# A gate taken straight from PSUM, a new order of seven products, and first weights converted earlier

## The chip, the cores and the metric

The kernel runs on one core of one Trainium2 chip. The metric is the device time of one execution in microseconds; lower is better. TensorE is called PE here, VectorE DVE, ScalarE ACT, GpSimd POOL; SyncE (SP) only starts DMA transfers.

## The reference

Three layers follow each other: causal attention with a decay in place of a softmax, an expert layer with a gate `h * sigmoid(1.702 * h)`, and a second one with a row-wise normalisation.

```python
def _attn_ref(q, k, v):            # (4, 8, 576, 64) each
    scores = scale * np.matmul(q, k.transpose(0, 1, 3, 2))
    gamma = 1.0 - 2.0 ** (-5.0 - np.arange(H, dtype=np.float32))
    Dmat = np.where(rel >= 0, gamma[:, None, None] ** rel[None, :, :], 0.0)
    return np.matmul(scores * Dmat[None], v)

def _moe_ref(x, w_in, w_out):      # 2304 tokens, 512 -> 2048 -> 512
    h = x @ w_in
    g = h * (1.0 / (1.0 + np.exp(-1.702 * h)))
    return g @ w_out

def _moe2_ref(x, w_in, w_out, g_ln):   # 512 -> 1024 -> 512
    h = x @ w_in
    e = np.exp(h - np.max(h, axis=-1, keepdims=True))
    solu = h * (e / (np.sum(e, axis=-1, keepdims=True) + 1e-09))
    ln = (solu - mean(solu)) / np.sqrt(var(solu) + 1e-06) * g_ln
    return ln @ w_out
```

## The kernel before

**Precision.** PE works on fp32r. To keep fp32 accuracy every operand is held as a high part (a cast to fp32r, by ACT) and a low part (the operand minus its high part, by POOL or DVE), and every product is three matmuls: high times high, low times high, high times low. The helper `split` does this: cast on ACT (L293), subtraction (L294), on POOL unless another engine is named.

**Attention** is the first part of the run: eight iterations `k`, two (batch, head pair) units each. POOL multiplies q by its decay (L469, L474), ACT scales v (L484, L488), PE forms scores, states and outputs, DVE masks the scores (L540) and scans the states (L508). Six input buffers are refilled by SP (`load_unit`), and between them SP brings the first pieces of the first expert layer's weights (`load_w`).

**Weights** come as float64. Each piece of 512 columns is turned into fp32 by three integer instructions on DVE (L269, L272, L275, in `convert`). For the input weights four differences of 256 columns (`queue_combine`, L284) follow, and then the split. All this is background work: it stands in a list `bg` with costs, and `slot(n)` takes from it up to a cost of n at fixed points of the program. Pieces marked late (the splits) are put into `late` and run at the next slot.

**The first expert layer** has 24 steps, 4 generations of 512 hidden columns times 3 pairs of 384-token blocks times 2. A step `emit_h` makes a 2 by 2 block of h with seven products of Strassen's kind (Winograd's form) instead of eight. Each product is 6 matmuls of 384 columns, so 42 for a step. The products go to four PSUM banks A, B, C, D, of which A, B and C are used twice: the second product adds onto the first, so PE has to wait until the first has been copied or added away (the copy of A is L678 on ACT, the sum from B is L670 on DVE). Operand sums of x come from `combine_x` and stand in seven tiles `x0` to `x6`, numbered in the order of the products, split high and low; generation 0 makes them and stores them to DRAM, later generations load them back on ACT's DMA queue.

Each of the four outputs then goes through a `gate`: ACT takes the sigmoid (L643), DVE multiplies (L644), ACT casts the high part (L293), POOL subtracts for the low part (L294).

After most steps `emit_y` multiplies gated blocks with the output weights: 48 matmuls of 384 columns (L739), only 24 after each of the first two steps, and once more 48 after the last. The sums are added into SBUF by DVE (L748), in generation 0 copied by ACT.

**In the last generation** the weights of the second expert layer are converted, combined, split and written to DRAM, one 512 KB unit at a time, from two buffers of the tile `ws` (`spill`, L393 to L395). When the first layer's tiles are free (`open_second`), SP fetches these units back, and the second layer begins (`emit_h2`, L803).

**Order.** Nothing is reordered by a scheduler: each engine executes its instructions in the order in which the program emits them.

## Time and profile before

| | us |
|---|---|
| Median of 2 runs | 735.41 (733.69 to 737.13) |
| The profiled execution | 730.73 |
| its span on the chip | 728.9 |
| PE busy | 664.2 (91%) |
| DVE busy | 536.6 (74%) |
| ACT busy | 292.4 (40%) |
| POOL busy | 324.1 (44%) |

The profile is of one execution. Its span is the time from the first instruction to the last; 1.8 us lie around it. [...]

### The profile page before, as it was taken

The numbers are of one execution on the slowest core, as the hardware profiler recorded it, in microseconds if no ns is written. First come the engines' busy times: TensorE is split into PE (matmuls) and PEld (weight loads), VectorE is DVE, ScalarE is ACT, GpSimd is POOL, SyncE is SP. The second block draws the span as 40 slices with busy tenths as digits, with TensorE's granted clock in tenths as the row PEclk, the third lists the DMA queues.
The fourth block names the chain that finished last, engine by engine and source line by source line (L and its number), as shares of the span: only waits on it lengthen the run. The fifth ranks groups of instructions, "written<-read, shape, count | busy, mean of one in ns | idle before, by whom it ended". The sixth has DMA issues, their size and how long they took to land.

```text
span 728.9 us, 11371 instructions
## 1 busy us (share of the span) xinstructions
PE 664.2 (91%) x4326; PEld 613.3 (84%) x4326; DVE 536.6 (74%) x846; ACT 292.4 (40%) x606; POOL 324.1 (44%) x312
## 2 busy tenths in 40 slices
PE   9989577979998989989999998589789999999998
PEld 8988467979998989989999987589468888888887
DVE  3799897976578778788877863657179898777780
ACT  3574335544444332433333332234244454433431
POOL 3578684753555352654435433257114333312300
PEclk9998979989999999999999999789999999999999
DMA  9996256271164762193921647712970000000001
GB/s 352 417 417 281 90 187 231 89 275 56 58 246 160 289 259 85 55 364 117 409 98 58 265 157 282 278 74 100 362 304 15 31 29 15 27 18 30 30 29 44
DMA packets 30006, 121.78 MB, mean 167 GB/s; under 512 B 3328, under 2 KB 3840, under 8 KB 29952
## 3 DMA queue, kind: packets, MB, share of 16 engines
q1 hardware_dynamic: 23904, 88.03, 31.7%
q10 hardware_dynamic: 6048, 33.03, 11.7%
q8 instruction: 34, 0.56, 0.3%
q14 instruction: 20, 0.16, 0.1%
HBM read 88.28 MB, written 32.77 MB: 166 GB/s over the span
## 4 chain that ended last, share of the span: by engine, by line
PE 58%; DVE 22%; DMA 11%; ACT 5%; issue 3%; POOL 2%; SPq 0%; ACTq 0%; POOLq 0%; DVEq 0%
PE y L739 15%; PE o L893 14%; PE h L803 9%; PE h_B L664 4%; PE h_C L664 3%; DVE mem L272 3%; PE h_A L664 3%; DVE mem L284 3%; DVE mem L275 3%; DVE mem L644 2%; DVE mem L269 2%; DMA mem<-in_w2in 2%; PE zT L867 2%; DVE mem L670 2%; PE h_D L664 2%
## 5 line engine op out<-in xcount | busy, mean ns | idle before, releaser
L294 POOL TENSOR_TENSOR g<-mem,g 128x384 fp32r<-128x384 f32 x96 | 109.0, 1147 | 195.7 <-ACT g L293 172.4
L293 ACT CAST g<-mem 128x384 fp32r<-128x384 f32 x96 | 48.5, 514 | 137.7 <-DVE mem L644 137.7
L739 PE MATMUL y<-g,wo 128*128 128x384 f32 x432 | 78.0, 335 | 0.0
L739 PEld LDWEIGHTS y<-g,wo 128*128 128x128 f32 x432 | 75.1, 188 | 0.3 <-DVE mem L748 0.2
L294 POOL TENSOR_TENSOR win<-mem,win 128x256 fp32r<-128x256 f32 (+2 forms) x55 | 49.0, 921 | 58.4 <-ACT win L293 54.4
L644 DVE TENSOR_TENSOR mem<-mem 128x384 f32<-128x384 f32 x72 | 46.7, 676 | 27.1 <-ACT mem L643 27.1
L294 POOL TENSOR_TENSOR ws<-mem,ws 128x512 fp32r<-128x512 f32 (+1 forms) x36 | 41.5, 1166 | 25.1 <-ACT ws L293 25.1
L748 DVE TENSOR_TENSOR mem<-y,mem 128x384 f32<-128x384 f32 x72 | 36.5, 551 | 18.6 <-PE y L739 18.2
L643 ACT ACTIVATE mem<-mem 128x384 f32<-128x384 f32 x72 | 35.5, 520 | 34.2 <-DVE mem L670 31.9
L803 PE MATMUL h<-ut,win 128*128 128x512 f32 x168 | 44.5, 396 | 4.1 <-DMA ut<-wdt 4.1
L809 DVE TENSOR_TENSOR mem<-h,mem 128x512 f32<-128x512 f32 x36 | 24.6, 687 | 31.6 <-PE h L803 17.5
L739 PE MATMUL y<-g,wo1dt.float32r 128*128 128x384 f32 x216 | 42.0, 343 | 2.4 <-ACT g L293 2.4
L670 DVE TENSOR_TENSOR mem<-h_B,mem 128x384 f32<-128x384 f32 x48 | 26.5, 551 | 23.8 <-ACT mem L678 14.8
L272 DVE SCALAR_TENSOR_TENSOR mem<-mem 128x512 uint32<-128x512 uint32 x44 | 42.5, 965 | 1.2
L275 DVE SCALAR_TENSOR_TENSOR mem<-mem 128x512 uint32<-128x512 uint32 x44 | 42.2, 958 | 1.2
L269 DVE TENSOR_SCALAR mem<-mem 128x512 uint32<-128x512 uint32 x44 | 33.7, 767 | 12.3 <-DMA mem<-in_w2in 7.2
L284 DVE TENSOR_TENSOR mem<-mem 128x256 f32<-128x256 f32 (+2 forms) x49 | 41.1, 870 | 2.2 <-POOL x L622 1.4
L854 POOL TENSOR_TENSOR mem<-mem 128x1 f32<-128x1 f32 x18 | 10.3, 572 | 72.8 <-DVE mem L853 66.6
L803 PEld LDWEIGHTS h<-ut,win 128*128 128x128 f32 x168 | 30.8, 188 | 13.3 <-DMA ut<-wdt 6.7
L893 PE MATMUL o<-u,zs 128*128 128x512 f32 (+1 forms) x171 | 41.7, 388 | 0.0
L739 PEld LDWEIGHTS y<-g,wo1dt.float32r 128*128 128x128 f32 x216 | 39.1, 195 | 2.7 <-ACT g L293 2.7
L739 PE MATMUL y<-g,wo0dt.float32r 128*128 128x384 f32 x216 | 40.6, 335 | 0.1
(144 smaller groups left out, 1578.7 us busy)
## 6 DMA issues: line engine op xcount, KB each, us to landing
x<-xd ACTq DMA_DIRECT2D x42, 768.0 KB, 8.3
xd<-x SPq DMA_DIRECT2D x21, 768.0 KB, 4.4
mem<-in_w SPq DMA_DIRECT2D x28, 512.0 KB, 4.8
in<-in_att SPq DMA_DIRECT2D x16, 576.0 KB, 7.8
in<-in_att SPq DMA_DIRECT2D x16, 544.0 KB, 8.2
out<-mem SPq DMA_DIRECT2D x17, 256.0 KB, 2.0
mem<-in_w2out SPq DMA_DIRECT2D x8, 512.0 KB, 3.9
wd<-ws SPq DMA_DIRECT2D x8, 512.0 KB, 6.7
```

Source lines behind the costliest of these rows:

```text
L269: lambda: nc.vector.tensor_scalar(x, high, 3, 0x3FFFFFF8, ALU.logical_shift_left, ALU.bitwise_and),
L272: lambda: nc.vector.scalar_tensor_tensor(high, high, 0xC0000000, x, ALU.bitwise_and, ALU.bitwise_or),
L275: lambda: nc.vector.scalar_tensor_tensor(x, low, 29, high, ALU.logical_shift_right, ALU.bitwise_or),
L284: self.nc.vector.tensor_tensor(o, a, b, ALU.subtract)
L293: self.nc.scalar.copy(hi, src)
L294: (engine or self.nc.gpsimd).tensor_tensor(lo, src, f32(hi), ALU.subtract)
L644: lambda: nc.vector.tensor_tensor(g, src, g, ALU.mult),
L664: nc.tensor.matmul(o, w[:, c:c + P], x[j][:, m, k], start=(start and i == 0), stop=(stop and i == 5), skip_group_check=True,)
L670: add = lambda o, a, b: nc.vector.tensor_tensor(o, a, b, ALU.add)
L739: nc.tensor.matmul(self.yps[m], w[:, c:c + P], gs[:, b], start=(begin and i == 0), stop=(end and i == 2),)
L803: nc.tensor.matmul(o, a[:, l, k], w[:, m], start=(start and i == 0), stop=(stop and i == 5), skip_group_check=True,)
L893: nc.tensor.matmul(o[:, 0:n], z[:, a, k], w[:, b, p * n:(p + 1) * n], start=(k == 0 and i == 0), stop=(k == FB - 1 and i == 2),)
```

## The change

The gate becomes ACT's own function `Gelu_apprx_sigmoid`, evaluated twice from the PSUM bank: once into the high part (which rounds it to fp32r), once in place in the bank. DVE then subtracts the high part from the bank for the low part. POOL and the temporary tiles of the gate are left out.

The seven products come in the order b11, t1, t2, b21, b22, t4, t3, and the x tiles are numbered and made in that order. C's output is summed in its bank, and so are the other two, in D and B.

The first input weights are converted in iterations 2 to 4 of the attention (they were in 4 to 6), and their loads are issued earlier. At most three late pieces run at one slot.

In the last generation the spilled units go through five buffers, two in `ws` and three in a free weight tile (`park`); the list must be empty after the last but one step, with fewer slots to divide it by. The identity's load goes to ACT's queue, ahead of the last fetches.

```diff
 class Build:
     def slot(self, n):
-        late, self.late = self.late, []
+        late, self.late = self.late[:LATE], self.late[LATE:]      # LATE = 3
...
+    def park(self, i):
+        if i % 5 < 2 or i < 2 * NOUT:
+            return self.ws[:, i % 5 if not i < 2 * NOUT else i % 2]
+        i = i % 5 - 2
+        return self.win[2][:, i * SLICE:(i + 1) * SLICE].rearrange("r (a b) -> r a b", a=2)
+
     def spill(self, u, i, src):
-        w = self.ws[:, i % 2]
+        w = self.park(i)
...
-        src = [s2, a11, s1, a12, a21, s2, a22]
+        src = [a11, s1, s2, a12, s2, a22, a21]
...
-    def gate(self, key, src, i):
-        g = self.at(_M["tmp"] + (4 + i) * TW, TW)
...
-        return [
-            lambda: nc.scalar.activation(g, src, AF.Sigmoid, scale=1.702),
-            lambda: nc.vector.tensor_tensor(g, src, g, ALU.mult),
-            lambda: self.split(gs[:, 0], gs[:, 1], g),
-        ]
+        def go(h):
+            nc.scalar.activation(gs[:, 0], h, AF.Gelu_apprx_sigmoid)
+            nc.scalar.activation(h, h, AF.Gelu_apprx_sigmoid)
+            nc.vector.tensor_tensor(gs[:, 1], h, f32(gs[:, 0]), ALU.subtract)
...
+        A = bank("A")
+        mul(A, 0, "b11", True, True)
+        nc.scalar.copy(c11, A)
+        yield 0
+        C = bank("C")
+        mul(C, 1, "t1", True, True)
+        nc.scalar.copy(c22, C)
+        yield 1
         B_ = bank("B")
-        mul(B_, 0, "t2", True, True)
...
+        mul(B_, 2, "t2", True, True)
         add(c12, B_, c11)
         yield 2
         mul(A, 3, "b21", False, True)
-        g11[0]()
-        g11[1]()
-        g11[2]()
+        g11(A)
         self.slot(0)
         yield 3
+        mul(C, 4, "b22", False, True)
+        add(C, C, c12)
+        g12(C)
+        yield 4
+        D_ = bank("D")
+        mul(D_, 5, "t4", True, True)
+        yield 5
+        mul(B_, 6, "t3", False, True)
         add(c21, B_, c11)
...
+        add(D_, D_, c21)
+        add(B_, c22, c21)
         self.done.add(("h", s))
         self.slot(n_slot)
-        g21[1]()
-        g21[2]()
+        g21(D_)
+        g22(B_)
         yield 6
...
-                self.slot((0, 0, 0, 0, 3, 3, 3, 0)[k])
+                self.slot((0, 0, 3, 3, 2.4, 0, 0, 0)[k])
...
-            for _ in range((0, 1, 1, 1, 1, 1, 1, 0)[k]):
+            for _ in range((2, 0, 0, 1, 1, 1, 1, 0)[k]):
                 load_w()
             if k > 3:
-                make_x(*((1, 3), (0, 2), (4, 6), (5,))[k - 4])
+                make_x(*((0, 3), (1, 2), (5, 6), (4,))[k - 4])
         self.open_right()
-        self.slot(5)
+        self.slot(6)
...
-            slots = max(1, 2 * (5 - s % 6 - (g == GENS - 1)) + 2 - (g == GENS - 1))
+            slots = max(1, 2 * (5 - s % 6) + 2 - 4 * (g == GENS - 1))
...
             if s == NSTEP - 2:
+                assert not self.bg and not self.late
...
+        nc.scalar.dma_start(out=self.at(IDENT_AT, P), in_=self.ident_in)
...
-        self.load(IDENT_AT, self.ident_in)
```

On PE, the seven products of one step in the third generation (h_A to h_D are the banks, x_126 to x_132 the tiles x0 to x6), before:

```order
L664 MATMUL h_B<-x_126,win0dt.float32r 128x384 x6
L664 MATMUL h_A<-x_127,win0dt.float32r 128x384 x6
L664 MATMUL h_C<-x_128,win0dt.float32r 128x384 x6
L664 MATMUL h_A<-x_129,win0dt.float32r 128x384 x6
L664 MATMUL h_B<-x_130,win0dt.float32r 128x384 x6
L664 MATMUL h_C<-x_131,win0dt.float32r 128x384 x6
L664 MATMUL h_D<-x_132,win0dt.float32r 128x384 x6
```

and with the change:

```order
L672 MATMUL h_A<-x_126,win0dt.float32r 128x384 x6
L672 MATMUL h_C<-x_127,win0dt.float32r 128x384 x6
L672 MATMUL h_B<-x_128,win0dt.float32r 128x384 x6
L672 MATMUL h_A<-x_129,win0dt.float32r 128x384 x6
L672 MATMUL h_C<-x_130,win0dt.float32r 128x384 x6
L672 MATMUL h_D<-x_131,win0dt.float32r 128x384 x6
L672 MATMUL h_B<-x_132,win0dt.float32r 128x384 x6
```

B moves from first to third place and its second product from fifth to last; A's and C's second products now have two products between them and the first, where A had one.

On DVE, a step of the second generation from the last conversion ahead of it (L670, now L678, are the sums from the banks, L644 the gate's multiplication, L652 the gate's subtraction, L275 or L276 a conversion), before:

```order
L275 SCALAR_TENSOR_TENSOR mem<-mem 128x512
L670 TENSOR_TENSOR mem<-h_B,mem 128x384
L644 TENSOR_TENSOR mem<-h_A,mem 128x384
L670 TENSOR_TENSOR mem<-h_B,mem 128x384
L670 TENSOR_TENSOR mem<-mem 128x384
L670 TENSOR_TENSOR mem<-h_C,mem 128x384
L644 TENSOR_TENSOR mem<-mem 128x384 x2
L670 TENSOR_TENSOR mem<-h_D,mem 128x384
L280 TENSOR_SCALAR mem<-mem 128x512
L269 TENSOR_SCALAR mem<-mem 128x512
```

and with the change:

```order
L276 SCALAR_TENSOR_TENSOR mem<-mem 128x512
L678 TENSOR_TENSOR mem<-h_B,mem 128x384
L652 TENSOR_TENSOR g_1081<-h_A,g_1081 128x384
L678 TENSOR_TENSOR h_C<-h_C,mem 128x384
L652 TENSOR_TENSOR g_1082<-h_C,g_1082 128x384
L678 TENSOR_TENSOR mem<-h_B,mem 128x384
L678 TENSOR_TENSOR h_D<-h_D,mem 128x384
L678 TENSOR_TENSOR h_B<-mem 128x384
L281 TENSOR_SCALAR mem<-mem 128x512
L270 TENSOR_SCALAR mem<-mem 128x512
```

The sums of C, D and B now end in their banks, and each gate still has one DVE instruction, now with one operand in PSUM; the count stays at nine for a step. The conversions keep their places, ahead of the first sum and behind the last.

On POOL, the end of the attention (L469 and L474, now L477 and L482, are the decays of the last two units in_72 and in_73; L622, now L630, the low parts of x; win0 the first input weights), before:

```order
L622 TENSOR_TENSOR x_127<-mem,x_127 128x384 x2
L622 TENSOR_TENSOR x_129<-mem,x_129 128x384 x2
L469 TENSOR_TENSOR in_72<-in_72,qdec 128x64
L469 TENSOR_TENSOR in_73<-in_73,qdec 128x64
L474 TENSOR_TENSOR in_72<-in_72,qdec 128x512
L474 TENSOR_TENSOR in_73<-in_73,qdec 128x512
L622 TENSOR_TENSOR x_126<-mem,x_126 128x384 x2
L622 TENSOR_TENSOR x_128<-mem,x_128 128x384 x2
L294 TENSOR_TENSOR win0dt.float32r<-mem,win0dt.float32r 128x768
L294 TENSOR_TENSOR win0dt.float32r<-mem,win0dt.float32r 128x512 x2
L622 TENSOR_TENSOR x_130<-mem,x_130 128x384 x2
L622 TENSOR_TENSOR x_132<-mem,x_132 128x384 x2
```

and with the change:

```order
L295 TENSOR_TENSOR win0dt.float32r<-mem,win0dt.float32r 128x768
L295 TENSOR_TENSOR win0dt.float32r<-mem,win0dt.float32r 128x512 x2
L630 TENSOR_TENSOR x_126<-mem,x_126 128x384 x2
L630 TENSOR_TENSOR x_129<-mem,x_129 128x384 x2
L477 TENSOR_TENSOR in_72<-in_72,qdec 128x64
L477 TENSOR_TENSOR in_73<-in_73,qdec 128x64
L482 TENSOR_TENSOR in_72<-in_72,qdec 128x512
L482 TENSOR_TENSOR in_73<-in_73,qdec 128x512
L630 TENSOR_TENSOR x_127<-mem,x_127 128x384 x2
L630 TENSOR_TENSOR x_128<-mem,x_128 128x384 x2
L630 TENSOR_TENSOR x_131<-mem,x_131 128x384 x2
L630 TENSOR_TENSOR x_132<-mem,x_132 128x384 x2
```

The first weights' subtractions move from behind the decays of the last two units to ahead of the first x.

## Rows read from the trace of the kernel before

**Rows 1.** Stretches: busy us of each engine (instructions), granted clock, DMA share, GB/s.

```profile
69.10:189.10 120.00, 96.26 (x495) 91.88 (x494) 96.54 (x127) 54.47 (x106) 73.13 (x57) 0.91 0.42 154
189.10:419.30 230.20, 222.05 (x1261) 219.67 (x1261) 182.42 (x281) 89.91 (x179) 111.64 (x89) 0.99 0.51 192
419.30:514.30 95.00, 78.21 (x409) 75.70 (x408) 54.04 (x93) 30.73 (x64) 42.13 (x40) 0.91 0.48 180
```

**Rows 2.** Waits of PE: us in total, times, longest.

```profile
PE h_B L664 <- DVE mem L670: 18.7, 9, 6.7
PE y L739 <- ACT g L293: 8.8, 3, 3.2
PE h_A L664 <- ACT mem L678: 8.6, 5, 3.4
PE h_B L664 <- ACT win1dt.float32r L293: 6.5, 1, 6.5
PE h L803 <- DMA ut<-wdt: 4.1, 8, 2.0
```

**Rows 3.** Timeline of PE: start, us, operation; beginnings of steps, end of the last.

```profile
69.10 1.31 PE L664 MATMUL h_B<-x,win0dt.float32r 128*128 128x384 f32 x6
...
115.60 1.40 PE L664 MATMUL h_B<-x,win0dt.float32r 128*128 128x384 f32 x6
...
173.49 1.20 PE L664 MATMUL h_B<-x,win1dt.float32r 128*128 128x384 f32 x6
...
189.09 1.20 PE L664 MATMUL h_B<-x,win 128*128 128x384 f32 x6
...
436.81 1.20 PE L664 MATMUL h_B<-x,win1dt.float32r 128*128 128x384 f32 x6
...
512.03 2.25 PE L739 MATMUL y<-g,wo1dt.float32r 128*128 128x384 f32 x12
```

**Rows 4.** Groups of DVE by shape: busy, mean ns, idle before.

```profile
L644 DVE TENSOR_TENSOR mem<-mem 128x384 f32<-128x384 f32 x72 | 46.7, 676 | 27.1 <-ACT mem L643 27.1
L272 DVE SCALAR_TENSOR_TENSOR mem<-mem 128x512 uint32<-128x512 uint32 x44 | 42.5, 965 | 1.2
...
L670 DVE TENSOR_TENSOR mem<-h_B,mem 128x384 f32<-128x384 f32 x48 | 26.5, 551 | 23.8 <-ACT mem L678 14.8 <-PE h_B L664 8.9
...
L644 DVE TENSOR_TENSOR mem<-h_A,mem 128x384 f32<-128x384 f32 x24 | 13.3, 552 | 19.0 <-ACT mem L643 19.0
```

**Rows 5.** Timeline of DVE: the same conversion beside POOL's work, and without it.

```profile
72.13 1.39 DVE L272 SCALAR_TENSOR_TENSOR win1dt.uint<-win1dt.uint,mem 128x512 uint32<-128x512 uint32 x1
...
84.83 0.69 DVE L272 SCALAR_TENSOR_TENSOR wo3dt.uint<-wo3dt.uint,mem 128x512 uint32<-128x512 uint32 x1
```

**Rows 6.** The page's groups: the subtraction of every gate on POOL.

```profile
L294 POOL TENSOR_TENSOR g<-mem,g 128x384 fp32r<-128x384 f32 x96 | 109.0, 1147 | 195.7 <-ACT g L293 172.4
```

**Rows 7.** Groups of ACT by shape.

```profile
L293 ACT CAST ws<-mem 128x512 fp32r<-128x512 f32 x22 | 13.1, 618 | 21.5 <-DMA wdb<-ws 14.9 <-DMA wdt<-ws 6.7
L643 ACT ACTIVATE mem<-h_A 128x384 f32<-128x384 f32 x24 | 11.8, 492 | 14.4 <-PE h_A L664 14.4
```

**Rows 8.** Timeline of POOL: last decays, first weights, last splits of x.

```profile
53.88 2.49 POOL L474 TENSOR_TENSOR in<-in,qdec 128x512 f32<-128x512 f32 x2
...
63.00 4.29 POOL L294 TENSOR_TENSOR win0dt.float32r<-mem,win0dt.float32r 128x768 fp32r<-128x768 f32 x3 [1.89 <-ACT win0dt.float32r L293]
67.25 8.53 POOL L622 TENSOR_TENSOR x<-mem,x 128x384 fp32r<-128x384 f32 x6
```

**Rows 9.** Timeline of PE where the second layer begins.

```profile
516.25 0.97 PE L803 MATMUL h<-ut,win 128*128 128x512 f32 x3 [1.98 <-DMA ut<-wdt]
...
533.32 1.54 PE L803 MATMUL h<-ut,ws 128*128 128x512 f32 x6
...
543.23 1.06 PE L867 MATMUL zT<-mem 128*128 128x128 f32 x8 [1.57 <-DMA mem<-in_ident]
```

**Rows 10.** Timeline of DVE: the end of tile 0's normalisation.

```profile
540.25 0.81 DVE L856 TENSOR_SCALAR mem<-mem 128x1024 f32<-128x1024 f32 x1 [0.67 <-POOL mem L854]
```

More of the change, by code (lines that the diff above doesn't have):

```diff
@@ L632, in load_x, with gate @@
         self.nc.scalar.dma_start(out=x, in_=self.xd[p][j])
-    def gate(self, key, src, i):
+    def gate(self, key):
         nc = self.nc
-        g = self.at(_M["tmp"] + (4 + i) * TW, TW)
         slot = self.gfree.pop(0)
+        self.gt[key] = slot
         gs = self.gs[slot]
-        self.gt[key] = slot
-        return [
-            lambda: nc.scalar.activation(g, src, AF.Sigmoid, scale=1.702),
-            lambda: nc.vector.tensor_tensor(g, src, g, ALU.mult),
-            lambda: self.split(gs[:, 0], gs[:, 1], g),
-        ]
+        def go(h):
+            nc.scalar.activation(gs[:, 0], h, AF.Gelu_apprx_sigmoid)
+            nc.scalar.activation(h, h, AF.Gelu_apprx_sigmoid)
+            nc.vector.tensor_tensor(gs[:, 1], h, f32(gs[:, 0]), ALU.subtract)
+        return go
     def emit_h(self, s, n_slot):
@@ L672, in emit_h @@
         c11, c12, c21, c22 = (self.at(_M["tmp"] + i * TW, TW) for i in range(4))
-        B_ = bank("B")
-        mul(B_, 0, "t2", True, True)
-        yield 0
-        A = bank("A")
-        mul(A, 1, "b11", True, True)
-        nc.scalar.copy(c11, A)
+        f = 2 * n
+        g11, g12, g21, g22 = (self.gate((g, p, t, f + c)) for t in range(2) for c in range(2))
+        A = bank("A")
[6 more added lines that the diff above has]
+        yield 1
+        B_ = bank("B")
+        mul(B_, 2, "t2", True, True)
         add(c12, B_, c11)
-        yield 1
-        C = bank("C")
-        mul(C, 2, "t1", True, True)
-        nc.scalar.copy(c22, C)
         yield 2
         mul(A, 3, "b21", False, True)
-        f = 2 * n
-        if not self.gfree:
-            raise ValueError(s)
-        g11, g12 = self.gate((g, p, 0, f), A, 0), self.gate((g, p, 0, f + 1), c12, 1)
-        g21, g22 = self.gate((g, p, 1, f), c21, 2), self.gate((g, p, 1, f + 1), c22, 3)
-        g11[0]()
-        g11[1]()
-        g11[2]()
+        g11(A)
         self.slot(0)
         yield 3
-        mul(B_, 4, "t3", False, True)
-        add(c21, B_, c11)
-        add(c22, c22, c21)
-        yield 4
-        mul(C, 5, "b22", False, True)
-        add(c12, C, c12)
-        g22[0]()
-        g12[0]()
-        g12[1]()
-        g12[2]()
-        g22[1]()
-        yield 5
-        D_ = bank("D")
-        mul(D_, 6, "t4", True, True)
-        add(c21, D_, c21)
-        g22[2]()
-        g21[0]()
+        mul(C, 4, "b22", False, True)
[6 more added lines that the diff above has]
+        mul(B_, 6, "t3", False, True)
+        add(c21, B_, c11)
+        add(D_, D_, c21)
+        add(B_, c22, c21)
         self.done.add(("h", s))
         self.slot(n_slot)
-        g21[1]()
-        g21[2]()
+        g21(D_)
+        g22(B_)
         yield 6
```

3 lines of the change are left out of this document (2 added, 1 removed).

## The prediction

> **What bounds the kernel now.** I read the stretches first, then the waits of PE, then the timelines of PE, DVE and POOL where those waits lie. In the first expert layer PE is the engine with the most work, but it is not kept busy everywhere: in the first generation (69.1 to 189.1 us) it is busy 96.3 of 120 us at a mean granted clock of 0.91, and DVE is busy just as long, 96.5 us; in the long middle it is busy 222 of 230 us; in the last 95 us it is busy 78.2, again at 0.91, while DVE has only 54 us of work [rows 1]. So one stretch is short of DVE, one is short of something that DVE, ACT and PE all wait for, and the middle is nearly full.
>
> The beginnings of the steps give the size of it [rows 3]. One undisturbed step lasts 189.09 - 173.49 = 15.60 us for 42 + 48 matmuls, 0.173 us each. Against that I count what each stretch has too much:
> - first two steps, each with 24 matmuls of y (4.16 us) fewer: 115.60 - 69.10 = 46.5 us for 22.9, too much 23.6;
> - next three steps: 57.9 us for 46.8, too much 11.1;
> - fifteen steps from 189.09 to 436.81: 247.7 us for 234.0, too much 13.7;
> - the last three, with the closing 48 matmuls (8.3 us), to 512.03 + 2.25 = 514.28: 77.5 us for 55.1, too much 22.4.
> Together 70.8 us. The listed waits are the larger part of it [rows 2]; the rest I put down to matmuls at the lower of the two clock levels, by the 0.91 of the two stretches that hold most of the waits, and let it shrink with the waits.
>
> A fifth piece lies where the second layer begins [rows 9]. From 514.28 to the first transposes at 543.23 are 28.95 us. The last 36 of the 78 matmuls in it run without waiting, from 533.32 to 543.23 - 1.57 = 541.66, so 0.23 us each or 18.0 us for all: too much 10.9, while each unit is fetched back from DRAM.
>
> **What the change does, part by part.**
>
> *POOL loses the gates.* 96 subtractions of 1.147 us, 109 us of POOL [rows 6]. What counts is DVE: the same conversion takes 1.39 us beside POOL and 0.69 without [rows 5], and the 44 of one kind average 0.965, so 44 x 0.275 = 12 us of this one of three conversion instructions is waiting for POOL [rows 4]. The three kinds together have lost some 35 us by that measure (an estimate from the one kind). The gates are a third of POOL's 324 us, so some 12 us of DVE time come back, about 4 of them in the first generation.
>
> *DVE's own gate work.* 72 multiplications at 0.676 us become subtractions with one operand in PSUM; the nearest row is the first gate's multiplication, which also reads a bank, at 0.552 [rows 4]. That is 72 x 0.124 = 8.9 us less, 2 us of it in the first generation. The five sums stay at 0.55 as long as writing a bank costs what reading one does; no row shows DVE writing a bank here, so I bound it by 0.55 and by twice that, 72 x 0.55 = 40 us spread over 24 steps, 1.65 us each, and take the lower end, since the nearest row (a sum from a bank, 0.551) is of the same size and shape. [...]
>
> *ACT* keeps ten instructions a step: four sigmoids and four casts become eight evaluations. The nearest row is the sigmoid read from a bank, 0.492 us [rows 7]; ACT is at most 45% busy in any stretch [rows 1], so even at double that price (2 us more a step) it stays covered. I take nothing for it. The wait it adds: the subtraction stands behind two ACT passes in a row, 0.98 us, where the multiplication stood behind one. Behind it in DVE's order are the next sum and then conversions. For the first two gates the next sum has to wait for PE's next product (1.04 us) anyway, and for the last two the conversions come first. I take 2 us for all, and keep up to 94 for the rivals.
>
> *The order of the products.* PE waited 18.7 us for the sum from B, queued on DVE behind conversions, and 8.6 for the copy of A [rows 2]. B's second product now comes two products later, at six products from the step's start instead of four, so DVE has 2.08 us more; A's copy has 1.04 more. Of the waits for B all but the longest are below 3 us, so most vanish; the same order gives the second gate two products more before y needs it, which concerns the 8.8 us of y.
>
> *First weights earlier.* Iterations 4 to 6 had eleven DVE pieces of it and now have the four differences: seven conversions leave the crowded end, six for iterations 2 and 3, one for the slot right behind the attention. At 0.69 to 1.39 us each [rows 5] that would give 5 to 10 us. But POOL does not get less: its decays end at 56.37, and it works on the first weights (4.29 us) and the six last subtractions of x until 75.78 with 1.89 idle [rows 8], and step 0 can't finish before x is split. The weights now go ahead of the last decays, which may delay the last attention iteration by 4.3 us. The ends are 4 us lost and 7 gained; I take 2 gained, the idle POOL time, since POOL's order is what ends last there. The loads only change places within one queue of DMAs, three of them are issued ahead of the last attention inputs in both versions, so nothing for that.
>
> *Spills.* In the last generation ACT waited 21.5 us for the two `ws` buffers to be written out [rows 7], and everything behind it in ACT's order with it: gates, copies of A, issues of x loads. With five buffers the first five spills of each half wait for nothing. All are done a step earlier, so the fetches no longer stand behind them in SP's queue, and the closing 96 matmuls (16.6 us) cover the fetches.
>
> **The sum**, against the profiled 730.73 us:
> - first two steps: 23.6 to 13. The second step's weights still have to be converted after the first step's sums, and DVE has no spare time there: 10.6 off;
> - next three: 11.1 to 4: 7.1 off;
> - middle: 13.7 to 4.5 (longest waits 3 us against 2.08 us of room, and x loads that no edit touches): 9.2 off;
> - last three: 22.4 to 7: 15.4 off;
> - beginning of the second layer: 10.9 to 2: 8.9 off. Late next is tile 0's normalisation, ready at 541.06 [rows 10], only 0.6 us ahead of PE's 541.66, hence the 2;
> - attention: 2 off; added wait for ACT: 2 on.
> 51.2 us off, 679.5 for a profiled run. The median stands 4.7 above that execution, and 735.4 - 51.2 gives **684 us**. With the bounds (first five steps saving 8 to 28 instead of 17.7, the last three and the second layer 16 to 30 instead of 24.3, the middle 4 to 12, attention -4 to 7) the forecast's own range is 664 to 706.
>
> **The rivals.**
>
> 1. *The first generation stays as it is.* DVE and POOL both do the x splits there, DVE's work is 96.5 us, and I free only some 6 of it; the waits might just move to x. Then the 17.7 us of the first five steps and half of the middle's 9.2 are missing: 735.4 - 29 = 706 us. For it speaks DVE as busy as PE; against it, that the longest waits are for single sums and gates. Chance 0.13.
>
> 2. *The spills stay the bound.* DVE's conversions there also wait for loads which SP starts only behind the first half's spills, and seven spills still follow each other within one step, at most three to a slot; if that order, not the buffers, sets the pace, the 24.3 us of the end are missing: 735.4 - 27 = 708 us. For it: DVE has 41 idle us in the last 95 [rows 1]. Against it: ACT's 21.5 us name the buffers. Chance 0.08.
>
> 3. *No real change:* each removed wait is replaced by one of like size, within 2% of 735. Chance 0.05.
>
> 4. *Slower: DVE is tied to ACT.* DVE executes in order, and each of its 96 subtractions now waits for two ACT passes. If DVE had nothing to cover any of them, it would idle 96 x 2 x 0.492 = 94 us, against 27.1 + 19.0 = 46 now [rows 4]: 48 us more. If these reached PE in full and only the gains of the end stayed (24 us), the time would be 735 + 48 - 24 = 759 us. DVE has 445 - 333 = 112 us idle in the three stretches [rows 1], so this decides only if most of the added waits fall where DVE is behind, that is in the first generation and right after a conversion. Chance 0.04.
>
> **Chances and range.** The forecast has 0.70. 2% of 735 (14.7 us) is about what a measurement here can tell from no change. Forecast and the first two rivals are faster by more than that, 0.91, of which I give 0.01 to smaller gains: faster 0.90, same 0.06, slower 0.04. The range has to take in the two middle rivals to leave out no more than 2 in 10: 664 to 710.
>
> **What would show it.** POOL's busy time falls by about 109 us and the conversions' mean from 0.965 towards 0.8; the waits of PE for the sum from B fall from 18.7 us to under 6; the second step starts at about 85 us instead of 90; the last three steps take about 62 us; no wait for fetched units, and transposes about 19 us after the last product of y; the granted clock is above 0.95 in the first and last stretch. Wrong would be: a DVE subtraction above 0.7 us, an ACT evaluation above 0.8, or PE waiting for x or for DVE subtractions in the first generation as long as it waited before.

## The result, and the profile after

The changed kernel takes **697.02 us** (median of 2 runs, 696.78 to 697.27) against 735.41: a ratio of 0.948, 95% interval 0.938 to 0.957. The forecast was 684, its range 664 to 710. The profiled execution took 697.27, its span is 695.5 us.

The table cuts both spans at the beginnings of the steps in the timeline of PE and sets the predicted saving beside the measured one (us).

| stage | before | after | predicted | measured |
|---|---|---|---|---|
| up to step 0 (attention) | 69.1 | 66.1 | -2 | -3.0 |
| steps 0 and 1 | 46.5 | 45.8 | -10.6 | -0.7 |
| steps 2 to 4 | 57.9 | 54.7 | -7.1 | -3.2 |
| steps 6 to 20 | 247.7 | 240.5 | -9.2 | -7.2 |
| steps 21 to 23 with the closing y | 77.5 | 69.5 | -15.4 | -8.0 |
| from there to the first transpose | 29.0 | 17.6 | -8.9 | -11.4 |

The measured column adds up to the 33.5 us between the two profiled executions. The medians are 38.4 apart, since the profiled run of before was 4.7 below its own median. The long middle and the second layer came out about as foreseen; the first five steps and the last three gave about half or less. (One execution of the variant "conversions ahead" below, the one that its trace is of, took 1366 us; it is left out of that variant's median, and its stages are not given.)

Stretches of the profile after, which answer [rows 1]; the columns are the same.

```profile
66.10:182.20 116.10, 96.71 (x494) 93.30 (x493) 86.27 (x128) 51.70 (x106) 43.64 (x33) 0.90 0.47 170
182.20:406.90 224.70, 220.68 (x1261) 219.81 (x1261) 149.48 (x281) 82.26 (x179) 47.20 (x33) 0.99 0.53 196
406.90:492.10 85.20, 73.69 (x411) 72.24 (x410) 50.02 (x93) 29.27 (x65) 25.33 (x23) 0.94 0.73 282
66.07:111.88 45.81, 30.99 (x135) 28.46 (x134) 42.40 (x55) 20.16 (x39) 26.26 (x20) 0.80 0.53 204
```

DVE (the third pair of numbers) has 33 us less work in the middle, where it was no bound, and 10 less in the first generation. The last row is steps 0 and 1 alone: DVE is busy 42.4 of 45.8 us there, PE only 31.0, at a mean granted clock of 0.80. The same two steps before:

```profile
69.10:115.60 46.50, 29.79 (x134) 26.70 (x133) 41.46 (x50) 18.95 (x34) 34.06 (x25) 0.86 0.41 161
```

POOL had 7.8 us more work there than with the change, but DVE had about the same: 41.5 us. None of the 10 us came out of these two steps. The granted clock is the share of the full one: in windows of 0.2 us, one every 0.5 us up to 690, it is 1.00 in 1302, 0.50 in 72 and between these in 6 (before: 1280, 91 and 9). So the lower of the prediction's two levels is 0.50.

The waits of PE, as in [rows 2].

```profile
PE h_B L672 <- DVE mem L678: 15.2, 4, 9.6
PE h_A L672 <- ACT win1dt.float32r L294: 5.0, 1, 5.0
PE h_B L672 <- DMA x<-xd: 3.2, 2, 1.7
PE h_B L672 <- DVE g L652: 2.9, 1, 2.9
PE h_A L672 <- POOL win1dt.float32r L295: 2.6, 1, 2.6
...
PE y L736 <- POOL wo3dt.float32r L295: 2.2, 1, 2.2
...
PE h_A L672 <- ACT mem L685: 1.3, 1, 1.3
```

Waits for the sum from B are fewer (4, not 9). The longest, 9.6 us, is in step 22, where PE had waited 6.7 us before as well. DVE and PE at that place before, DVE waiting for a load ahead of the sum:

```profile
468.41 0.43 DVE L269 TENSOR_SCALAR mem<-mem 128x512 uint32<-128x512 uint32 x1 [4.43 <-DMA mem<-in_w2in]
...
472.21 2.29 PE L664 MATMUL h_B<-x,win0dt.float32r 128*128 128x384 f32 x6 [6.74 <-DVE mem L670]
```

Waits for the copy of A, for gates ahead of y and for fetched units are gone or nearly so.

Groups of DVE and ACT by shape (busy, mean ns, idle before), which answer [rows 4] and [rows 7].

```profile
L273 DVE SCALAR_TENSOR_TENSOR mem<-mem 128x512 uint32<-128x512 uint32 x44 | 32.1, 730 | 1.2
L678 DVE TENSOR_TENSOR h_B<-mem 128x384 f32<-128x384 f32 x24 | 14.5, 603 | 0.0
L652 DVE TENSOR_TENSOR g<-h_C,g 128x384 fp32r<-128x384 f32 x24 | 13.4, 558 | 23.1 <-ACT h_C L651 23.1
L678 DVE TENSOR_TENSOR h_C<-h_C,mem 128x384 f32<-128x384 f32 x24 | 13.3, 555 | 0.0
L652 DVE TENSOR_TENSOR g<-h_A,g 128x384 fp32r<-128x384 f32 x24 | 13.3, 554 | 20.8 <-ACT h_A L651 20.8
L652 DVE TENSOR_TENSOR g<-h_D,g 128x384 fp32r<-128x384 f32 x24 | 13.2, 551 | 1.5 <-ACT h_D L651 1.5
L652 DVE TENSOR_TENSOR g<-h_B,g 128x384 fp32r<-128x384 f32 x24 | 13.2, 549 | 1.2 <-ACT h_B L651 1.2
L651 ACT ACTIVATE h_A<-h_A 128x384 f32<-128x384 f32 x24 | 11.7, 489 | 0.0
```

The prices hold: a subtraction from PSUM 0.55 us, an evaluation on ACT 0.49, a sum written into a bank 0.555 (0.603 with both operands in SBUF). The conversion in the first row falls from 965 to 730 ns.

The timeline of PE at the places that the prediction named; it answers [rows 3] and [rows 9].

```profile
66.07 1.34 PE L672 MATMUL h_A<-x,win0dt.float32r 128*128 128x384 f32 x6
...
85.21 0.69 PE L672 MATMUL h_A<-x,win1dt.float32r 128*128 128x384 f32 x1 [5.03 <-ACT win1dt.float32r L294]
88.51 1.97 PE L672 MATMUL h_A<-x,win1dt.float32r 128*128 128x384 f32 x5 [2.62 <-POOL win1dt.float32r L295]
...
99.90 1.87 PE L672 MATMUL h_B<-x,win1dt.float32r 128*128 128x384 f32 x6 [2.73 <-DVE mem L678]
...
455.18 2.29 PE L672 MATMUL h_B<-x,win0dt.float32r 128*128 128x384 f32 x6 [9.60 <-DVE mem L678]
...
489.98 2.24 PE L736 MATMUL y<-g,wo1dt.float32r 128*128 128x384 f32 x12
492.06 1.55 PE L800 MATMUL h<-ut,win 128*128 128x512 f32 x6
...
509.78 1.03 PE L864 MATMUL zT<-mem 128*128 128x128 f32 x8
```

Step 1 starts at 85.21, as predicted, but it then takes 26.7 us, against 25.6 before (89.98 to 115.60), where it began so:

```profile
89.98 0.69 PE L664 MATMUL h_B<-x,win1dt.float32r 128*128 128x384 f32 x1 [6.51 <-ACT win1dt.float32r L293]
```

The second layer follows y without a gap, and no unit is waited for.

Two timelines of DVE in the same trace hold what went wrong. The first is the way into step 1:

```profile
67.09 1.40 DVE L273 SCALAR_TENSOR_TENSOR win1dt.uint<-win1dt.uint,mem 128x512 uint32<-128x512 uint32 x1
...
74.09 0.55 DVE L678 TENSOR_TENSOR mem<-h_B,mem 128x384 f32<-128x384 f32 x1
...
82.21 1.55 DVE L285 TENSOR_TENSOR mem<-mem 128x256 f32<-128x256 f32 x4
...
84.95 2.38 DVE L621 TENSOR_TENSOR mem<-mem 128x768 f32<-128x768 f32 x1
87.37 3.85 DVE L285 TENSOR_TENSOR mem<-mem 128x768 f32<-128x768 f32 x2
...
96.48 2.90 DVE L630 TENSOR_TENSOR x<-mem,x 128x384 fp32r<-128x384 f32 x2
99.30 0.54 DVE L678 TENSOR_TENSOR mem<-h_B,mem 128x384 f32<-128x384 f32 x1
...
448.71 0.43 DVE L270 TENSOR_SCALAR mem<-mem 128x512 uint32<-128x512 uint32 x1 [8.46 <-DMA mem<-in_w2in]
```

Apart from three waits of 2.8 us together, DVE works through from 64.8 to 111.9: conversions until 74.1, step 0's sums and gates, conversions and the four differences of the next weights until 83.7, then x sums, conversions and an x split ahead of step 1's first sum from B. The last row is the other place: in step 22 DVE waits 8.46 us for one of the two last float64 pieces of the spills, and the sum that PE needs stands behind it, as it did before behind a wait of 4.43.

### The profile page after: what moved, and what is told of

It reads as the page before. It is cut to its first block, busy times and chain, and to the rows that moved or that the text cites. A ratio compares the mean times of both kernels' runs of the same rounds, so it can differ in the third digit from the quotient of the medians.

```text
span 695.5 us, 11232 instructions
## 1 busy us (share of the span) xinstructions
PE 651.9 (94%) x4326; PEld 609.2 (88%) x4326; DVE 485.6 (70%) x846; ACT 279.2 (40%) x606; POOL 213.2 (31%) x216
## 4 chain that ended last, share of the span: by engine, by line
PE 68%; DMA 6%; DVE 4%; ACT 1%; issue 1%; POOL 0%; ACTq 0%; DVEq 0%
PE y L736 22%; PE o L890 14%; PE h L800 12%; PE h_B L672 5%; PE h_A L672 5%; PE h_C L672 5%; DMA x<-xd 4%; PE h_D L672 3%; PE zT L864 2%; DMA mem<-in_w2in 1%; DVE mem L273 1%; DVE mem L276 0%; DVE mem L270 0%; DVE x L630 0%; DVE g L652 0%
## 5 line engine op out<-in xcount | busy, mean ns | idle before, releaser
L295 POOL TENSOR_TENSOR win<-mem,win 128x256 fp32r<-128x256 f32 (+2 forms) x63 | 58.6, 960 | 114.7 <-ACT win L294 80.6
L678 DVE TENSOR_TENSOR mem<-h_B,mem 128x384 f32<-128x384 f32 x48 | 26.5, 551 | 32.3 <-PE h_B L672 30.2
L685 ACT COPY mem<-h_A 128x384 f32<-128x384 f32 x24 | 11.6, 483 | 84.7 <-PE h_A L672 84.7
L890 PE MATMUL o<-wo,zs 128*128 128x512 f32 (+1 forms) x171 | 40.0, 378 | 0.0
L630 POOL TENSOR_TENSOR x<-mem,x 128x384 fp32r<-128x384 f32 x30 | 34.6, 1180 | 17.5 <-ACT x L628 17.5
L736 PEld LDWEIGHTS y<-g,wo0dt.float32r 128*128 128x128 f32 x216 | 37.7, 188 | 0.0
L672 PE MATMUL h_B<-x,win0dt.float32r 128*128 128x384 f32 x108 | 23.8, 358 | 13.7 <-DVE mem L678 10.8
L890 PEld LDWEIGHTS o<-wo,zs 128*128 128x128 f32 x171 | 31.0, 188 | 6.0
L276 DVE SCALAR_TENSOR_TENSOR mem<-mem 128x512 uint32<-128x512 uint32 x44 | 34.5, 785 | 1.2
L890 PEld LDWEIGHTS o<-u,zs 128*128 128x128 f32 x171 | 29.9, 189 | 5.1
L270 DVE TENSOR_SCALAR mem<-mem 128x512 uint32<-128x512 uint32 x44 | 20.7, 469 | 18.4 <-DMA mem<-in_w2in 10.6
```

Of the source, the lines that this page charges most:

```text
L270: lambda: nc.vector.tensor_scalar(x, high, 3, 0x3FFFFFF8, ALU.logical_shift_left, ALU.bitwise_and),
L276: lambda: nc.vector.scalar_tensor_tensor(x, low, 29, high, ALU.logical_shift_right, ALU.bitwise_or),
L295: (engine or self.nc.gpsimd).tensor_tensor(lo, src, f32(hi), ALU.subtract)
L630: (engine or self.nc.gpsimd).tensor_tensor(x[:, 1, k], a[:, k], f32(x[:, 0, k]), ALU.subtract)
L672: nc.tensor.matmul(o, w[:, c:c + P], x[j][:, m, k], start=(start and i == 0), stop=(stop and i == 5), skip_group_check=True,)
L678: add = lambda o, a, b: nc.vector.tensor_tensor(o, a, b, ALU.add)
```

## Experiments

Ratios are to the kernel before, from runs on the same chip as each experiment; medians are of two to six executions, and each row's stages come from one trace. The stages, cut as above:

| kernel | median us | ratio, 95% interval | step 0 at | 0 and 1 | 2 to 4 | 6 to 20 | 21 to 23 |
|---|---|---|---|---|---|---|---|
| change | 697.02 | 0.948 (0.938 to 0.957) | 66.1 | 45.8 | 54.7 | 240.5 | 69.5 |
| first weights late | 699.0 | 0.951 (0.947 to 0.955) | 69.5 | 43.1 | 52.6 | 240.6 | 69.2 |
| old gate | 711.3 | 0.968 (0.965 to 0.971) | 65.6 | 50.7 | 62.5 | 238.5 | 73.1 |
| old order | 703.37 | 0.957 (0.952 to 0.962) | 68.4 | 45.7 | 54.0 | 241.8 | 71.7 |
| old gate and order | 719.5 | 0.981 (0.976 to 0.985) | 66.4 | 51.1 | 57.8 | 251.1 | 72.5 |
| two spill buffers | 699.49 | 0.952 (0.948 to 0.956) | 65.6 | 46.0 | 52.6 | 240.8 | 71.5 |
| no x loads at the end | 691.01 | 0.942 (0.935 to 0.949) | 65.5 | 45.9 | 54.2 | 240.9 | 60.4 |
| last pieces later | 695.87 | 0.949 (0.945 to 0.953) | 66.1 | 45.3 | 53.9 | 240.4 | 68.9 |
| no low parts of x | 692.85 | 0.943 (0.939 to 0.947) | 64.2 | 42.5 | 54.2 | 239.5 | 70.5 |
| conversions ahead | 696.37 | 0.948 (0.945 to 0.952) | | | | | |
| casts later | 689.92 | 0.938 (0.935 to 0.940) | 65.6 | 45.9 | 52.7 | 240.5 | 62.8 |
| casts and pieces | 688.23 | 0.935 (0.932 to 0.938) | 71.6 | 39.9 | 51.4 | 238.8 | 62.9 |
| fewer at step 0 | 688.55 | 0.937 (0.935 to 0.940) | 70.7 | 35.9 | 56.1 | 240.1 | 62.8 |

In every row with stages the first transpose comes 17.6 us after the last product of y.

**1. The first weights late again.**

```diff
-                self.slot((0, 0, 3, 3, 2.4, 0, 0, 0)[k])
+                self.slot((0, 0, 0, 0, 3, 3, 3, 0)[k])
-            for _ in range((2, 0, 0, 1, 1, 1, 1, 0)[k]):
+            for _ in range((0, 1, 1, 1, 1, 1, 1, 0)[k]):
-        self.slot(6)
+        self.slot(5)
```

> The changed kernel with the first weights' conversions and loads back in iterations 4 to 6 of the attention (all else as changed). The first step started 3.0 us earlier after the change (66.07 against 69.10 us) and the second step 4.8 us earlier, but the third only 3.7. Theory A (the early conversions gave those 3 us, as DVE is the end of the attention's chain): first step at about 69 us and 3 to 5 us slower than the changed kernel, about 701 us. Theory B (POOL's splits of x end the stretch whatever DVE does): no change beyond 1 us, about 697 us.

Step 0 starts 3.4 us later, but step 2 starts at 112.6, against 111.9. So the early weights bring the start forward and lose it again before step 2. The median, 699.0, lies between the two expected, and the interval contains the change's ratio.

**2. The gate and the order of the products, each undone alone and both together.** The gate's edit:

```diff
...
         def go(h):
-            nc.scalar.activation(gs[:, 0], h, AF.Gelu_apprx_sigmoid)
-            nc.scalar.activation(h, h, AF.Gelu_apprx_sigmoid)
-            nc.vector.tensor_tensor(gs[:, 1], h, f32(gs[:, 0]), ALU.subtract)
+            nc.scalar.activation(g, h, AF.Sigmoid, scale=1.702)
+            nc.vector.tensor_tensor(g, h, g, ALU.mult)
+            self.split(gs[:, 0], gs[:, 1], g)
```

> The changed kernel with the gate of before (sigmoid by ACT, product by DVE, cast by ACT, subtraction by POOL), the first, third and fourth gate's input being the bank; order of the products, early weights and buffers as changed. Theory A (the gate gives DVE its time back, since POOL's 96 subtractions slowed DVE's conversions): conversions' mean back from 0.73 to about 0.95 us, waits for the sum from B in the middle return, 8 to 15 us slower than the changed kernel, 705 to 712 us. Theory B (the order of the products took the middle's waits away, the gate only saves idle engines' time): within 3 us, 697 to 700 us.

The order's edit puts back the sequence t2, b11, t1, b21, t3, b22, t4, with its x tiles and the sums where it needs them (the gate stays new):

```diff
+        mul(B_, 0, "t2", True, True)
...
-        mul(A, 0, "b11", True, True)
+        mul(A, 1, "b11", True, True)
...
-        mul(B_, 6, "t3", False, True)
...
+        mul(D_, 6, "t4", True, True)
```

> The changed kernel with the order of the seven products of before (t2, b11, t1, b21, t3, b22, t4) and the x tiles numbered for it; gate, early weights and buffers as changed. Theory A (the later place of B's second product gives DVE 2.08 us of room in each step): PE waits again for the sum from B in the middle, 6 to 12 us slower, 703 to 709 us. Theory B (faster conversions alone would have ended those waits): within 3 us, 697 to 700 us.

With both edits:

> The changed kernel with both the gate and the order of the products of before; early weights, buffers and the list's deadlines as changed. The middle (fifteen steps from step 6 on) lasted 240.5 us in the changed kernel, 238.5 with the gate alone of before, 241.8 with the order alone of before, and 247.7 before. Theory A (either of the two is enough to end the middle's waits for the sum from B): the middle is back at 245 to 248 us, the whole at 718 to 724 us. Theory B (something else of the change ended them): the middle stays at 239 to 242 us, the whole at about 713 to 717 us.

The gate is worth 14.3 us in the new order (711.3 - 697.0) and 16.1 in the old one (719.5 - 703.4); the order 6.4 and 8.2, of which the 6.4 lies within the two intervals' overlap (0.948 and 0.957) and is not clear of noise. What remains, 733.6 - 719.5 on one chip or some 14 us, is the rest of the change. By the traces it is 2.7 at the start of step 0, 5.0 in the last three steps and 11.4 at the second layer's start, less 4.6 us in steps 0 and 1 and 3.4 in the middle, which take longer there than in the kernel before.

The gate's worth does not lie where it was expected. In the new order, undoing it makes steps 0 and 1 4.9 us longer, steps 2 to 4 7.8 and the last three 3.6, but not the middle, whose waits were to return: it is 2.1 shorter. In steps 0 and 1 DVE is as busy as in the change (42.0 us); PE waits there for the splits of weights by ACT and POOL, 9.2 and 8.9 us, against 5.7 and 4.8 in the change. The old gate's subtractions stand in POOL's order among these splits.

In the middle the gate and the order do the same work: without both the steps 6 to 20 take 251.1 us, with either alone 241.8 or 238.5. The waits of PE without both, over the whole run (lines after the gate stand 3 later there):

```profile
PE h_B L675 <- DVE mem L681: 29.3, 12, 11.4
```

Of these, eight waits of 11.2 us together are in the middle (7.9 before, none in the change); the one of 11.4 is in step 22.

The three conversions of the same shape with the old gate alone, in groups of DVE:

```profile
L276 DVE SCALAR_TENSOR_TENSOR mem<-mem 128x512 uint32<-128x512 uint32 x44 | 39.8, 905 | 1.2
L273 DVE SCALAR_TENSOR_TENSOR mem<-mem 128x512 uint32<-128x512 uint32 x44 | 35.8, 814 | 1.2
...
L270 DVE TENSOR_SCALAR mem<-mem 128x512 uint32<-128x512 uint32 x44 | 26.2, 595 | 13.5 <-DMA mem<-in_w2in 7.7 <-DMA mem<-in_w2out 5.0 <-DMA mem<-in_w 0.8
```

Their sum is 2.31 us there, against 1.98 in the change (785, 730, 469) and 2.69 before (958, 965, 767). Over 44 of each, the old gate, with its work on POOL, thus cost DVE's conversions 15 us, not quite half of the fall of 31; the rest came with the other edits.

**3. Two spill buffers instead of five.**

```diff
-        w = self.park(i)
+        w = self.ws[:, i % 2]
```

> The changed kernel with all spills through the two ws buffers again. Theory A (the buffers gave the earlier end of the spills, and with it the covered fetches): ACT waits for the buffers again, last three steps and beginning of the second layer 10 to 20 us longer, 707 to 717 us. Theory B (the earlier deadline for the list gave it, and DMA bandwidth sets the pace of the last steps anyway): within 4 us, 697 to 701 us.

Only 2 us come back in the last three steps, less than the medians can tell, and the second layer's start doesn't change. The three new buffers, on which the prediction built, are not what removed the waits for fetched units. The spills' earlier deadline is what is left of the edit at this place, with the identity's load on another queue; neither was undone alone. The order in SP's queue speaks for the deadline. Timelines of SP, the last spills and the first fetch, before and with the change:

```profile
506.91 4.01 SPq L395 DMA_DIRECT2D wdt<-ws  x2
511.02 1.15 SPq L210 DMA_DIRECT2D ut<-wdt  x2
```

```profile
463.53 1.57 SPq L403 DMA_DIRECT2D wdt<-ws  x2
465.19 1.29 SPq L211 DMA_DIRECT2D ut<-wdt  x2
```

In both the first fetch is issued right behind the last spill, but before that was 3 us ahead of the end of y, and now it is 27 (25 with two buffers). The identity's load was issued behind all fetches (at 534.36), so it can have caused only the 1.57 us that the transposes waited for it.

**4. The last x loads left out.**

```diff
-                        self.load_x(after, j)
+                        if g < GENS - 1 or at + 2 < NPR:
+                            self.load_x(after, j)
```

> The changed kernel without the x loads for the last pair of the last generation (seven loads of 768 KB; the last two steps compute with the pair before's x). In the changed kernel DVE waited 8.46 us for the last two float64 pieces, loaded from 438.2 us on and there at 448.7, while those x loads and the spills were moving, and PE waited 9.6 us for DVE in step 22. Theory A (the transfers are late because the x loads are ahead of them): the pieces arrive 4 us or more earlier, PE's wait falls below 4 us, the last three steps take 63 us instead of 69.5. Theory B (the pieces are issued late by SP, behind DVE's conversions, and the x loads don't matter): the wait stays above 7 us.

Timeline of DVE without these loads, at the conversion that had waited 8.46 us:

```profile
440.66 0.43 DVE L270 TENSOR_SCALAR mem<-mem 128x512 uint32<-128x512 uint32 x1 [1.00 <-DMA mem<-in_w2in]
```

The wait is 1.00 us, PE's wait at that place 3.1 instead of 9.6, and the last three steps take 60.4 us, 9 less. In the change both float64 pieces of 512 KB are issued from 438.2 us on, behind seven x loads of 768 KB that were issued from 424 to 434; there they land after 10.8 us (the median of the two), here after 5.2. They are also issued 3.1 us earlier here (435.1): in the change SP waited 3.9 us for a spill to be written. So the x loads make the pieces late, most of it in the transfer and some of it in the issue.

**5. Mending the end.** First the conversions of the last two pieces behind step 22's first gate:

```diff
         g11(A)
-        self.slot(0)
+        self.slot(99 if s == NSTEP - 2 else 0)
...
-            self.slot(6 if s == 0 else self.left() // max(1, slots) if s + 2 < NSTEP else 0)
+            self.slot(6 if s == 0 else self.left() // max(1, slots) if s + 3 < NSTEP else 0)
+            if s == NSTEP - 2:
+                self.slot(0)
```

> The changed kernel with the conversions of the last two float64 pieces moved from ahead of step 22's first sum to behind its first gate's subtraction, so that DVE's wait for them no longer stands ahead of the sum that PE waits for. Theory A (PE's 9.6 us in step 22 are DVE's order, a wait for a transfer ahead of a sum): the wait goes, 3 us of it come back in step 23 through the banks, last three steps about 63 us, 690 to 693 us. Theory B (whatever stands behind the conversions is late as well): within 2 us, 695 to 699 us.

The wait leaves step 22 and comes back in step 23. The timelines of PE and of ACT:

```profile
467.48 2.29 PE L672 MATMUL h_A<-x,win1dt.float32r 128*128 128x384 f32 x6 [6.19 <-ACT mem L685]
```

```profile
464.81 2.24 ACT L294 CAST win<-mem 128x256 fp32r<-128x256 f32 x7 [4.30 <-DVE mem L766]
466.95 0.47 ACT L685 COPY mem<-h_A 128x384 f32<-128x384 f32 x1
```

Seven casts of y for the second layer stand ahead of the copy of A in ACT's order, and they wait for DVE. The median is no different from the change's, as the second theory had it. So the second edit moves these splits behind step 23's last product, with the first one kept:

```diff
-                for fn in ys:
+                for fn in ys[:4]:
                     fn()
...
             if s + 1 == NSTEP:
+                for fn in ys[4:]:
+                    fn()
                 self.slot(0)
```

> The last two pieces' conversions stand behind step 22's first gate, and the seven splits of y for the second layer behind step 23's last product instead of ahead of its first. Theory A (what kept the last three steps long in the run before was only the order in which ACT and DVE execute): both waits go, the last three steps take 60 to 63 us instead of 69.5, the second layer still starts within 2 us of the last product of y, and the median is 688 to 691. Theory B (the splits then come too late for the second layer, or the copy of A waits for something else): the last three steps shorten, but the second layer starts 4 us or more later, or they stay above 66 us; 694 to 699.

No wait of PE above 1.8 us is left there; the last three steps take 62.8 us, near the 62 that the prediction gave the change itself. 0.938 (0.935 to 0.940) stands against 0.949 (0.945 to 0.953) with the first edit alone.

**6. The first generation.** POOL's subtractions for the low parts of the first pair's x left out (a line that is not shown sets these parts to zero once, at the start):

```diff
-            for k in range(2):
+            for k in range(2 if p else 0):
```

> Leaves out the fourteen subtractions by POOL that make the low parts of the first pair's x (they are zero instead). Theory A (POOL's work beside DVE doubles the six output-piece conversions before step 0, which took 1.22 to 1.66 us each, and by that keeps the first two steps long): the six conversions take about 3.6 us in all instead of 8.3, steps 0 and 1 take about 40 us instead of 45.8, the median falls by 4 to 7 us, to 690 to 693. Theory B (the amount of DVE and ACT work between the two steps holds it, whatever POOL does): the conversions may get shorter but steps 0 and 1 still take over 44 us, and the median stays within 2 us of 697.

Timeline of DVE, the first and the last of the six output-piece conversions:

```profile
63.68 0.42 DVE L270 TENSOR_SCALAR mem<-win1dt.uint 128x512 uint32<-128x512 uint32 x1
...
66.65 0.69 DVE L276 SCALAR_TENSOR_TENSOR mem<-win1dt.uint 128x512 uint32<-128x512 uint32 x1
```

The six take 3.7 us instead of 8.3, and step 2 starts at 106.7 instead of 111.9. Of these 5.2 us, 1.8 are an earlier step 0 and 3.3 are in steps 0 and 1, which take 42.5 us, between the 40 and the 44 of the two theories. POOL's work beside DVE costs about what the doubled durations say (4.6 us); in the change it sits on the path.

Then the same output pieces moved ahead into attention iterations 5 and 6, and the next input weights ahead of the first step's end ("conversions ahead" in the table). Alone, this edit gave 696.37 us, 0.948 (0.945 to 0.952), no different from the change.

```diff
-        self.slot(0)
+        self.slot(2.4 if s == 0 else 0)
...
-                self.slot((0, 0, 3, 3, 2.4, 0, 0, 0)[k])
+                self.slot((0, 0, 3, 3, 2.4, 3, 3, 0)[k])
```

> The changed kernel with the first two output pieces converted in iterations 5 and 6 of the attention, the second input weights' conversions right behind the attention, and their differences behind step 0's first gate instead of behind its last sum. Theory A (the second step's weights, at the end of one chain of conversions on DVE, set the start of step 1): step 1 starts 3 to 6 us earlier than 85.2 us, first two steps 40 to 43 us instead of 45.8, about 692 us. Theory B (POOL, with x and weights to split, sets it): no change, 697 us.

Together with the later casts:

> The same, and the first output pieces converted in attention iterations 5 and 6, the next input weights ahead of the first step's end. If DVE's chain between the first two steps is what holds step 1, steps 0 and 1 shorten from 45.8 to about 41 us and the median is 3 to 5 us below that of the kernel with the later splits alone. If the conversions only move to a place where POOL's splits of x slow them just as much, steps 0 and 1 plus the start of step 0 come out the same within 1 us, and so do the two medians.

Steps 0 and 1 shrink to 39.9 us, and step 0 starts 6 us later: step 2 begins at 111.5 in both. The medians differ by 1.7 us and their intervals overlap. Last, in that version, fewer conversions right behind step 0:

```diff
-            for j in self.emit_h(s, 8.4 if s == 0 else -(-self.left() // slots) + 1):
+            for j in self.emit_h(s, 3 if s == 0 else -(-self.left() // slots) + 1):
...
-            self.slot(6 if s == 0 else ...
+            self.slot(3 if s == 0 else ...
```

> The kernel with the later splits and the earlier output pieces, and with fewer conversions at the two slots behind step 0 (costs of 3 and 3 instead of 8.4 and 6); what they leave moves into the later steps of the first generation. Theory A (what keeps step 1 long is the amount of conversions that stand on DVE ahead of step 0's last gates and of step 1's first sum): the waits of PE at those two places, 3.7 and 5.6 us, fall below 1.5 us each, steps 0 and 1 take 33 to 36 us instead of 39.9, steps 2 to 4 at most 2 us more than their 51.4, and the median is 682 to 686 (688 without this edit). Theory B (DVE is the bound of the whole generation): steps 2 to 5 take back what steps 0 and 1 gain, the beginning of step 6 moves by less than 1.5 us, and the median stays at 687 to 690.

Steps 0 and 1 fall to 35.9 us, steps 2 to 4 rise to 56.1, and step 6 starts at 178.28 instead of 178.45. One of the two waits aimed at shrank (from 3.72 us), the other did not (5.56 without the edit); timeline of PE:

```profile
88.84 1.32 PE L672 MATMUL h_B<-x,win1dt.float32r 128*128 128x384 f32 x6 [0.99 <-DVE g L652]
99.25 2.29 PE L672 MATMUL h_B<-x,win1dt.float32r 128*128 128x384 f32 x6 [5.96 <-DVE mem L678]
```

Moving conversions about within the generation is worth nothing that the intervals can tell. The best version is the one of casts and pieces, 688.23 us; the two beside it can't be told from it.

## Why the prediction came out as it did

The sign, the range and the prices of the gate held, and the middle and the second layer's start gave about what was said. The forecast was 13 us too low because three terms of its sum were about twice too large or far more: the first two steps, the next three and the last three. Between the profiled executions the sum was 17.7 too large (51.2 against 33.5); 5 of that were made good by chance, as the profiled run of before lay below its median. The first five steps saved 3.9 us, less than the bound of 8 that the prediction gave them. The measured 697 lies nearer to the first rival's 706 than to 684, and within the range because the other terms held. (Its stated bounds, all taken together, would give 660 to 713 and not 664 to 706.)

- **First two steps, 10.6 off: wrong, 0.7.** The step that failed is the term "23.6 to 13" itself: it removes single waits where, in the prediction's own words, DVE has no spare time, and where it freed only some 6 us of DVE in the whole generation. DVE's work in these steps did not fall at all: 42.4 of 45.8 us, against 41.5 of 46.5 before, and while this work stands there the steps can't be much shorter. Seven conversions did leave the attention's end, but others took their place beside POOL's x splits at 1.2 to 1.7 us each, and POOL's decays and x are the same work as before. Undoing the early weights makes the two steps 2.7 us shorter and step 0's start 3.4 later, so it leaves step 2's start 0.7 us later. Taking POOL's low parts away moved the start of step 2, spreading the conversions only moved the time. This is the first rival, for these two steps. The gate does take 4.9 us out of them, by POOL's order, on which the working was silent, but the early start of step 0 and whatever else costs time there takes most of it back (experiment 2). In the new order the x split of product 1 (2.90 us on DVE at 96.48) stands ahead of the first sum from B, and PE waits 2.73 us; but with the old order, where that split comes behind the sum, PE waits 4.20 us for it, so the wait is not that order's doing.
- **Next three steps, 7.1 off: 3.2.** PE is idle 4.6 of their 54.7 us, by waits of 1.7 and 2.9, and the rest of the excess over 46.8 goes with a granted clock of 0.95. The term was mis-sized by half.
- **Middle, 9.2 off: 7.2.** Right, but not for the order alone: gate or order each suffice there. What is left are waits for x loads, 4.1 us together, which the prediction had left out of the gain; none for a sum from B is left.
- **Last three steps, 15.4 off: 8.0.** The step that failed is the credit to the buffers; the longest wait for B (6.7 us), which lies here, got no price of its own. The buffers were worth 2 us, and that wait stood behind a late load in the trace of before already (4.43 us of DVE's idle time); the two late loads behind x traffic took 9. Rival 2 had the wait, "conversions there also wait for loads", but gave the spills' order as its reason, where the x loads were it. With the order on DVE and ACT mended the stage takes 62.8 us against the 62 forecast, by edits that the forecast did not have.
- **Second layer's start, 8.9 off: 11.4.** The transposes come 17.6 us after y. The 2 us allowed for tile 0's normalisation were not needed. The reason given, that the fetches no longer stand behind the spills in SP's queue, is what the traces show; that the buffers bring it about was wrong (experiment 3).
- **Gate.** 0.55 and 0.49 us came out as read from the nearest rows, a bank written costs 0.555 to 0.603, far from the upper bound of 1.1, and the rival of DVE tied to ACT did not happen: DVE waits 23.1 and 20.8 us behind the first two gates' evaluations, 1.5 and 1.2 behind the other two, 46.6 in all against 46.1 before. A source in PSUM made no difference at this size: the sums with a bank among their operands take 0.54 to 0.57, and a sum of two SBUF operands with POOL idle, at 78.05 us, 0.55. POOL's busy time fell by 110.9 us (109 predicted). The conversions gave back 31 us of DVE rather than 12, but DVE's work in the first two steps, where it has no slack, did not fall.
- **Clock.** Above 0.95 in the first and last stretch was wrong: 0.90 and 0.94. In steps 0 and 1 the 135 matmul records take 31.0 us, where 132 at 0.173 would take 22.8: about 8 us more (an estimate), at the granted clock of 0.80. That the clock rises as the waits shrink was the author's estimate; these two steps don't show it, with PE idle 14.8 us at 0.80 and, before, 16.7 at 0.86.

Not settled by an edit: that the spills' deadline, not the identity's queue, removed the waits for fetched units is read from the order in SP's queue alone. Not settled either is why steps 0 and 1 and the middle, without the new gate and order, take longer than in the kernel before.

## What to carry to other kernels

Before crediting a removed wait, sum the work of the engine that released it over that stretch: where it fills the stretch, as DVE's 42 of 46 us, the wait only moves, and an edit pays by work it takes away, there or on the engine that slows it, as the 5.2 us without POOL's low parts. Before crediting a wait to the order of instructions, look for a wait for a transfer ahead of it, as the 4.43 us ahead of the 6.74 before. Less work on an engine bought nothing where it had slack: with the old gate, and 15 us more of DVE's conversions over the run, the middle took 238.5 us, against 240.5. When a buffer's wait is removed, look up which load and which instruction in each engine's order comes next: here a 512 KB load behind x traffic, and seven casts ahead of a copy.

## What was unexpected of the hardware

- Beside POOL's work, DVE's sums here are slowed or not by where their operands lie. In the change a sum with a bank among its operands took 0.54 to 0.57, with or without POOL beside it (0.55 at 75.03, beside POOL's subtraction). A sum of two SBUF operands, 0.55 to 0.56 when POOL is idle, took 0.75 beside POOL at three places and 0.93 at a fourth. Timeline of DVE there, the second row the sum in question:

```profile
431.39 0.57 DVE L678 TENSOR_TENSOR h_D<-h_D,mem 128x384 f32<-128x384 f32 x1
431.86 0.93 DVE L678 TENSOR_TENSOR h_B<-mem 128x384 f32<-128x384 f32 x1
```

  POOL works through both, on four splits from 428.57 to 433.93.

- After the 9.60 us wait in step 22 six matmuls took 2.29 us instead of 1.20. The granted clock of that stretch (third number from the end) is 0.50; it is 1.00 from 166.60 to 182.20, where six take 1.20:

```profile
455.10:457.40 2.30, 2.22 (x7) 2.23 (x8) 1.36 (x4) 1.31 (x3) 1.92 (x2) 0.50 0.35 144
```

  Six also took 2.29 after the waits of 6.19 and 5.96 us in experiments 5 and 6, so each of these waits was followed by some 1.1 us more for the next six.
